# Local and global attention with a top-80 expert layer: PSUM banks by head, 32-row tiles for the global keys, longer q/k rows, and other places for the gate stage, the zeros and the late weights

## The chip, the core and the metric

The kernel runs on one core of a Trainium2 chip. The metric is the time in microseconds that one launch takes on the device; lower is better. The page called the profile is one execution of the program recorded by the hardware. In it PE is TensorE (the matrix engine), PEld its weight loads, DVE is VectorE, ACT is ScalarE, POOL is GpSimd and SP is SyncE, which here only issues transfers. L346 means line 346 of the kernel.

## What is computed

Attention comes first. In each of 8 batches, 8 heads have 32 global and 512 local tokens of width 64. A global query sees all 544 keys. A local query sees the 32 global keys and the local keys at most 32 positions away. The 4352 output rows of 512 values go through a layer of 8 experts: each token picks the expert with the largest gate logit, each expert keeps the 80 tokens with the highest gate weights, and all other rows of the output are zero.

```python
s_g = scale * q_g @ k_all.T ;  out_g = softmax(s_g) @ v_all          # k_all: global, then local keys
s_ll = where(|i - j| <= 32, scale * q_l @ k_l.T, -1e9)
s_l = concat([scale * q_l @ k_g.T, s_ll]) ;  out_l = softmax(s_l) @ concat([v_g, v_l])
x = concat([out_g, out_l]) as (8 * 544, 512)
logits = x @ w_gate ;  e = argmax(logits) ;  g = softmax(logits)[e]
for each expert e:                       # keeps its 80 largest g
    out[tok] = g[tok] * (relu(x[tok] @ w1[e]) @ w2[e])     # w1: 512 x 1024, w2: 1024 x 512
```

## The kernel before

The unit of work is a **quad**, four heads of one batch: 16 quads, two for each batch. The loop below handles quad q, while it loads, transposes and computes logits for later ones. `some(n)` runs up to n waiting steps of the top-80 search (each a VectorE maximum-of-8 and a replacement), and the functions from `La` to `Ld` form the gate stage of a finished batch. The main parts, with cuts marked by `...`:

```python
    def load_qk(q):
        b, qd = divmod(q, 2)
        qks[q] = lpool.tile([P, 2, 4, 4, D], FP32, tag="qk", name=f"qk{q}")
        for t, src in ((0, q_l), (1, k_l)):
            nc.sync.dma_start(
                out=qks[q][:, t].rearrange("p h i d -> p h (i d)"),
                in_=src[b, 4 * qd:4 * qd + 4].rearrange("h (p i) d -> p h (i d)", i=4))
    ...
    def regroup(q, t):
        if t == 0:
            qkr[q] = lpool.tile([P, 2, 4, 4, D], FP16, tag="qkr", name=f"qkr_{q}")
        nc.scalar.copy(out=qkr[q][:, t].rearrange("p i h d -> p h i d"), in_=qks[q][:, t])
    ...
    def T_chunk(q, j):
        b, qd = divmod(q, 2)
        buf = qkT[(2 * q + j) % 4]
        T_ps = psT([P, 2, 512], FP16, f"T_ps{q}_{j}")
        for t in range(2):
            for i in range(4):
                nc.tensor.transpose(out=T_ps[:, t, 128 * i:128 * i + 128],
                                    in_=qkr[q][:, t, i, 2 * j:2 * j + 2, :],
                                    identity=ident16[:, :])
        dst = buf[:, 0:1088].rearrange("x (t y) -> x t y", t=2)[:, :, 0:512]
        nc.scalar.copy(out=dst.rearrange("x t (p i) -> x t p i", i=4),
                       in_=T_ps[:].rearrange("x t (i p) -> x t p i", i=4))
        nc.scalar.copy(out=kO[(2 * q + j) % 4][:],
                       in_=buf[:, 576:1088].rearrange("x (u w y) -> x u w y", w=2, y=64)[:, :, ::-1, :])
    ...
    def L_fill(q, j):
        s = st.setdefault(q, {"eL": [], "eQ": []})
        buf = qkT[(2 * q + j) % 4]
        l_ps = [psS([P, 512], FP32, f"l_ps{q}_{j}_{hh}") for hh in range(2)]
        ko = kO[(2 * q + j) % 4]
        for t in range(8):
            for hh in range(2):
                o = 64 * hh
                if t % 2 == 0:
                    lhsT = buf[o:o + 64, 512 + 64 * t:640 + 64 * t]
                else:
                    lhsT = ko[o:o + 64, t // 2].rearrange("x w y -> x (w y)")
                nc.tensor.matmul(out=l_ps[hh][:, 64 * t:64 * t + 64], lhsT=lhsT,
                                 rhs=buf[o:o + 64, 64 * t:64 * t + 64], start=True, stop=True)
        for hh in range(2):
            eL = hpool.tile([P, 512], FP32, tag="eL", bufs=8, name=f"eL{q}_{j}_{hh}")
            nc.scalar.activation(out=eL[:], in_=l_ps[hh][:], func=AF.Exp, scale=scale)
            s["eL"].append(eL)
    ...
    def mask(q, j):
        for hh in range(2):
            eng = nc.vector if hh == 0 else nc.gpsimd
            eL = st[q]["eL"][2 * j + hh]
            eng.tensor_tensor(out=eL[:], in0=eL[:], in1=band[:].rearrange("p t i -> p (t i)"), op=ALU.mult)
    ...
    def H_chunk(q, u):
        b, qd = divmod(q, 2)
        s = st[q]
        v = vb[q % 3]
        o = psO([P, 4, 65], FP32, f"o_ps{q}_{u}")
        nc.tensor.matmul(out=o[:].rearrange("p h d -> p (h d)"), lhsT=s["eG"][:, 128 * u:128 * u + 128],
                         rhs=vbd[b % 2][:, qd].rearrange("p h d -> p (h d)"), start=True, stop=False,
                         skip_group_check=True)
        for h in range(4):
            for odd in range(2):
                t = 2 * u + odd
                nc.tensor.matmul(out=o[64 * odd:64 * odd + 64, h, :],
                                 lhsT=s["eL"][h][:, 64 * t:64 * t + 64],
                                 rhs=v[:, 5 * odd + u, h, :], start=False, stop=True,
                                 skip_group_check=True)
        rec = hpool.tile([P, 4], FP32, tag="rec", bufs=4, name="rec")
        nc.vector.reciprocal(out=rec[:], in_=o[:, :, 64])
        nc.vector.tensor_tensor(out=s["xn"][:, u].rearrange("p (h d) -> p h d", h=4), in0=o[:, :, 0:64],
                                in1=rec[:].unsqueeze(2).to_broadcast([P, 4, 64]), op=ALU.mult)
    ...
    def best(g):
        if g < 2:
            lst = spool.tile([NB * E, cap], FP32, tag="lst", bufs=1, name=f"lst{g}")
            yield from rounds(scT[g][:], lst[:])
            cand = spool.tile([E, NB, cap], FP32, tag="cand", bufs=1, name=f"cand{g}")
            def move():
                for s in range(NB):
                    nc.sync.dma_start(out=cand[:, s, :], in_=lst[8 * s:8 * s + 8, :])
            yield move
            R[g] = spool.tile([E, cap], FP32, tag=f"R{g}", bufs=1, name=f"R{g}")
            yield from rounds(cand[:].rearrange("e s r -> e (s r)"), R[g][:])
    ...
    for q in range(NQ):
        ...                                   # load_qk(q + 4), load_v(q + 2)
        H_chunk(q, 0)
        ...                                   # T_chunk(q+2, 0), La, L_fill(q+1, 0), mask, regroup, shift_v
        some(1)
        H_chunk(q, 1)
        ...                                   # Lb1, L_fill(q+1, 1), T_chunk(q+2, 1), Lb2, mask
        some(1)
        H_chunk(q, 2)
        ...                                   # Lb3, some(more), G_fill, Q_fill, regroup
        H_chunk(q, 3)
        ...                                   # Lc, some(1), Q_chunk, Q_fill, C_chunk, X_chunk x2, some(more), Ld
        if q < 4 * NRES:                      # NRES = 3 experts, a half-megabyte piece for each quad
            ...
            load_w(e, (k,))
        if q >= 1:
            zeros(1)                          # half a megabyte of the zero rows of the output
        ...                                   # from quad 14: expert 3 and half of 4, into the V buffers
```

`C_chunk` is the cast of a quad's output on GpSimd (line 392), `G_fill` and `Q_fill` compute logits with the global keys and the global queries, `shift_v` copies V moved by 64 rows, `X_chunk` transposes the output on TensorE and copies it to xT on VectorE. After the loop stand the gate stage of the last batch, what is left of the search, the final ten rounds, the threshold, the row numbers (`idx`), a gather of 80 rows for each expert, and the experts (the products `rv` and the counts `jt`, between threshold and row numbers, are in the diff below):

```python
    def fh(e):
        hTs[e] = rpool.tile([P, 8, cap], BF16, tag="fhT", bufs=2, name=f"fhT{e}")
        for half in range(2):
            h_ps = psO([P, 4, cap], FP32, f"h_ps{e}{half}")
            for f in range(4):
                for cc in range(4):
                    o = 512 * half + 128 * f
                    nc.tensor.matmul(out=h_ps[:, f, :], lhsT=w1sb[e][:, cc, o:o + 128], rhs=xTs[e][:, cc, :],
                                     start=(cc == 0), stop=(cc == 3))
            nc.scalar.activation(out=hTs[e][:, 4 * half:4 * half + 4, :], in_=h_ps[:], func=AF.Relu, scale=1.0)
    ...
        nc.gpsimd.indirect_dma_start(out=out,
                                     out_offset=bass.IndirectOffsetOnAxis(ap=idx[:, e:e + 1], axis=0),
                                     in_=y[:], in_offset=None, bounds_check=N - 1, oob_is_err=False)
```

## Time and profile before

| | us |
|---|---|
| measured time, median of three | 336.25 (335.89 to 336.62) |
| span of the profiled execution | 335.5 |
| TensorE matmuls busy | 218.9 (65%) |
| TensorE weight loads busy | 155.6 (46%) |
| VectorE busy | 207.6 (62%) |
| ScalarE busy | 146.4 (44%) |
| GpSimd busy | 149.3 (44%) |
| hardware queue (q1), share of 16 DMA engines | 44.7%, 41.30 MB, 72128 packets |
| software queue (q0), share of 16 DMA engines | 33.7%, 18.80 MB, 13984 packets |

The busy shares are means over the whole span. No engine is busy for two thirds of it, yet the shares change much from one stage to the next, so they have to be read by stage. Matmuls overlap in the array, so a TensorE that is busy isn't one at its peak. A packet is one contiguous row of a transfer: 1 KB for q and k, 256 bytes for V. The software queue is the one that GpSimd issues: weights (read as f32, written as bf16), the gather and the scatters.

### The profile page before, as it was taken

What the parts mean: (1) busy time and instruction counts of PE and PEld (TensorE: products, weight loads), DVE (VectorE), ACT (ScalarE), POOL (GpSimd) and SP (SyncE); (2) the same over time, 40 slices, a digit from 0 to 9 for tenths busy, and PEclk for the clock granted to TensorE, in tenths of its full rate; (3) what the DMA queues carried; (4) which work ended last, traced back from release to release, by engine and by line L of the source; (5) the groups of instructions that cost most, each with busy time, mean ns of one, the idle gap of its engine ahead of it and who ended that gap; (6) DMA issues with size and microseconds to landing.
All of it is one profiled execution on the core that took longest, in us unless ns stands there. A gap on an engine that the chain in (4) does not pass through costs nothing. (4 is left out here: it accounts for less than half of the span.)

```text
span 335.5 us, 8730 instructions
## 1 busy us (share of the span) xinstructions
PE 218.9 (65%) x3510; PEld 155.6 (46%) x3510; DVE 207.6 (62%) x597; ACT 146.4 (44%) x241; POOL 149.3 (44%) x200
## 2 busy tenths in 40 slices
PE   1206989887889889788684878769551013049960
PEld 0105766664666666465463456446330002047730
DVE  4303565857855675688839599989958878012320
ACT  4158977595687679375563455230000000013300
POOL 6014656763754681663644144453172125532231
PEclk9998699999999999989898599995855555559996
DMA  7787899699899899999879714204999999960211
GB/s 206 189 198 252 203 236 252 161 251 198 222 216 271 215 231 212 264 220 274 221 163 292 134 53 127 86 4 93 220 164 212 270 209 207 209 133 21 61 39 39
DMA packets 86151, 60.64 MB, mean 181 GB/s; under 512 B 50144, under 2 KB 79200, under 8 KB 86112
## 3 DMA queue, kind: packets, MB, share of 16 engines
q1 hardware_dynamic: 72128, 41.30, 44.7%
q0 software_dynamic: 13984, 18.80, 33.7%
q8 instruction: 27, 0.44, 0.5%
q14 instruction: 12, 0.10, 0.1%
HBM read 62.19 MB, written 14.70 MB: 229 GB/s over the span
## 5 line engine op out<-in xcount | busy, mean ns | idle before, releaser
L329 POOL TENSOR_TENSOR eL<-eL,band 128x512 f32<-128x512 f32 x32 | 40.9, 1278 | 42.5 <-ACT eL L322 41.0
L329 DVE TENSOR_TENSOR eL<-eL,band 128x512 f32<-128x512 f32 x32 | 27.4, 855 | 41.0 <-ACT eL L322 41.0
L275 ACT COPY qkT<-T_ps 128x1024 f16<-128x1024 f16 x32 | 32.6, 1018 | 42.9 <-PE T_ps L271 37.9
L352 PEld LDWEIGHTS o_ps<-vb,eL 128*64 128x64 f32 x1024 | 37.1, 143 | 26.1 <-issue 20.6
L352 PE MATMUL o_ps<-vb,eL 128*64 128x65 f32 x1024 | 46.5, 234 | 2.4 <-POOL vb L188 1.4
L346 PE MATMUL o_ps<-vbd,eG 128*128 128x260 f32 x128 | 45.6, 440 | 0.0
L322 ACT ACTIVATE eL<-l_ps 128x512 f32<-128x512 f32 x64 | 34.7, 597 | 9.6 <-PE l_ps L318 9.6
L145 ACT CAST qkr<-qk 128x1024 f16<-128x1024 f32 x32 | 33.4, 1046 | 12.2 <-DMA qk<-in_q_l_dram 10.7
L777 ACT ACTIVATE fhT<-h_ps 128x320 bf16<-128x320 f32 x16 | 6.9, 437 | 64.0 <-PE h_ps L775 63.6
L392 POOL CAST xb<-xn 128x1024 bf16<-128x1024 f32 x16 | 16.6, 1036 | 29.7 <-DVE xn L358 29.6
L271 PE MATMUL T_ps<-ident,qkr 128*128 128x128 f16 x256 | 22.8, 240 | 10.6 <-ACT qkr L145 7.5
L384 PE MATMUL x_ps<-identf,xn 128*128 128x128 f32 x128 | 22.1, 309 | 11.4 <-DVE xn L358 11.4
L358 DVE TENSOR_TENSOR xn<-o_ps,rec 128x256 f32<-128x256 f32 x64 | 27.2, 425 | 3.2
L283 POOL COPY qkT<-kgp 128x32 f16<-128x32 f16 x32 | 7.9, 249 | 41.2 <-ACT qkT L275 33.9
L318 PE MATMUL l_ps<-qkT 64*128 64x64 f16 x256 | 14.5, 200 | 16.1 <-POOL qkT L283 10.0
L271 PEld LDWEIGHTS <-qkr 128*128 128x128 f16 x256 | 16.9, 107 | 13.1 <-ACT qkr L145 8.6
L384 PEld LDWEIGHTS x_ps<-identf,xn 128*128 128x128 f32 x128 | 15.8, 156 | 13.9 <-DVE xn L358 13.5
L387 DVE COPY xT<-x_ps 128x512 f32<-128x512 f32 x32 | 20.6, 684 | 2.2 <-PE x_ps L384 1.9
L187 POOL COPY vb<-vb 64x1040 f32<-64x1040 f32 x16 | 17.0, 1062 | 10.4 <-DMA vb<-in_v_l_dram 10.4
L346 PEld LDWEIGHTS o_ps<-vbd,eG 128*128 128x128 f32 x128 | 20.6, 202 | 1.2
L303 ACT ACTIVATE eQ<-gq_ps 128x320 f32<-128x320 f32 x32 | 13.9, 435 | 16.6 <-PE gq_ps L300 16.5
L318 PEld LDWEIGHTS <-qkT 64*128 64x128 f16 x256 | 10.2, 99 | 22.9 <-issue 11.2
(138 smaller groups left out, 433.1 us busy)
## 6 DMA issues: line engine op xcount, KB each, us to landing
out_dram<-zt SPq DMA_DIRECT2D x17, 512.0 KB
qk<-in_q_l_dram SPq DMA_DIRECT2D x16, 512.0 KB
qk<-in_k_l_dram SPq DMA_DIRECT2D x16, 512.0 KB
w2sb<-in_moe_w_dram POOLq DMA_DIRECT2D x14, 512.0 KB, 20.8
vb<-in_v_l_dram SPq DMA_DIRECT2D x48, 128.0 KB
w1sb<-in_moe_w_dram POOLq DMA_DIRECT2D x12, 512.0 KB, 20.9
x_scr<-xb SPq DMA_DIRECT2D x8, 514.0 KB
vb<-in_moe_w_dram POOLq DMA_DIRECT2D x6, 512.0 KB, 7.2
```

Of the source, the lines that this page charges most:

```text
L145: nc.scalar.copy(out=qkr[q][:, t].rearrange("p i h d -> p h i d"), in_=qks[q][:, t])
L187: nc.gpsimd.tensor_copy(out=v[0:64, 5:9], in_=v[0:64, 1:5])
L271: nc.tensor.transpose(out=T_ps[:, t, 128 * i:128 * i + 128], in_=qkr[q][:, t, i, 2 * j:2 * j + 2, :], identity=ident16[:, :])
L275: nc.scalar.copy(out=dst.rearrange("x t (p i) -> x t p i", i=4), in_=T_ps[:].rearrange("x t (i p) -> x t p i", i=4))
L318: nc.tensor.matmul(out=l_ps[hh][:, 64 * t:64 * t + 64], lhsT=lhsT, rhs=buf[o:o + 64, 64 * t:64 * t + 64], start=True, stop=True)
L322: nc.scalar.activation(out=eL[:], in_=l_ps[hh][:], func=AF.Exp, scale=scale)
L329: eng.tensor_tensor(out=eL[:], in0=eL[:], in1=band[:].rearrange("p t i -> p (t i)"), op=ALU.mult)
L346: nc.tensor.matmul(out=o[:].rearrange("p h d -> p (h d)"), lhsT=s["eG"][:, 128 * u:128 * u + 128], rhs=vbd[b % 2][:, qd].rearrange("p h d ...
L352: nc.tensor.matmul(out=o[64 * odd:64 * odd + 64, h, :], lhsT=s["eL"][h][:, 64 * t:64 * t + 64], rhs=v[:, 5 * odd + u, h, :], start=False, ...
L358: nc.vector.tensor_tensor(out=s["xn"][:, u].rearrange("p (h d) -> p h d", h=4), in0=o[:, :, 0:64], in1=rec[:].unsqueeze(2).to_broadcast([P ...
L384: nc.tensor.transpose(out=x_ps[:, 128 * u:128 * u + 128], in_=s["xn"][:, u, 128 * j:128 * j + 128], identity=identf[:, :])
L387: nc.vector.tensor_copy(out=xT[:], in_=x_ps[:])
```

## The change

**Heads and banks.** A quad's accumulators are laid out by head instead of by block of 128 queries, one PSUM bank for each head. The global keys were one matmul over all four heads with a block-diagonal V of 260 columns; they become 16 matmuls on tiles of 32 rows of the array, each with its own 65 columns and bank. A head's outputs need only that head's masked logits, so heads 0 and 2 can start when the first half of the logits is there.

**Loads.** q and k come in rows of 2 KB (8 tokens) instead of 1 KB. w2 is read with four neighbouring rows on a partition, for which fh takes w1's columns with a step of four.

**Engines.** The kO copies go from ScalarE to GpSimd, half of the xT copies from VectorE to ScalarE; in the last quads GpSimd takes all masks and ScalarE part of the normalization.

**Gate stage and search.** The gate stage of a batch is spread over two quads. The lists of the first two groups of batches are merged before one second search, which had been done for each. The products `rv` are made for each batch in the loop.

**Late loads.** Zeros move to quads 10 and later. The weights of two and a half experts instead of one and a half go into buffers that the loop sets free (the q/k buffers, then the V buffers). The scatters are declared independent of one another.

The core of the diff, with cuts marked by `...`:

```diff
-        qks[q] = lpool.tile([P, 2, 4, 4, D], FP32, tag="qk", name=f"qk{q}")
         for t, src in ((0, q_l), (1, k_l)):
-            nc.sync.dma_start(
-                out=qks[q][:, t].rearrange("p h i d -> p h (i d)"),
-                in_=src[b, 4 * qd:4 * qd + 4].rearrange("h (p i) d -> p h (i d)", i=4))
+            hs = src[b, 4 * qd:4 * qd + 4].rearrange("(g a) (p i) d -> (a p) g (i d)", a=2, i=8)
+            nc.sync.dma_start(out=qkb[q % 2][:, t].rearrange("p g i d -> p g (i d)"), in_=hs)
     def regroup(q, t):
         if t == 0:
-            qkr[q] = lpool.tile([P, 2, 4, 4, D], FP16, tag="qkr", name=f"qkr_{q}")
-        nc.scalar.copy(out=qkr[q][:, t].rearrange("p i h d -> p h i d"), in_=qks[q][:, t])
+            qkr[q] = lpool.tile([P, 2, 8, 2, D], FP16, tag="qkr", name=f"qkr_{q}")
+        nc.scalar.copy(out=qkr[q][:, t].rearrange("p i g d -> p g i d"), in_=qkb[q % 2][:, t])
...
+    def T_chunk(q, t):
+        T_ps = psT([P, 8, 2, 64], FP16, f"T_ps{q}_{t}")
+        for i in range(8):
+            nc.tensor.transpose(out=T_ps[:, i].rearrange("x a p -> x (a p)"),
+                                in_=qkr[q][:, t, i].rearrange("p g d -> p (g d)"), identity=ident16[:, :])
+        dst = qkT[q % 2][:, :, 544 * t:544 * t + 512].rearrange("x a (p i) -> x a p i", i=8)
+        nc.scalar.copy(out=dst, in_=T_ps[:].rearrange("x i a p -> x a p i"))
+    def kg_copy(q):
+        b, qd = divmod(q, 2)
+        nc.gpsimd.tensor_copy(out=qkT[q % 2][:, :, 512:544], in_=kgp[:, b, 2 * qd:2 * qd + 2, :])
+    def kO_copy(q):
+        for a in range(2):
+            (nc.gpsimd.tensor_copy if q < 14 else nc.scalar.copy)(
+                out=kO[q % 2][:, a],
+                in_=qkT[q % 2][:, a, 576:1088].rearrange("x (u w y) -> x u w y", w=2, y=64)[:, :, ::-1, :])
...
-            s["eL"].append(eL)
+            s["eL"][2 * hh + j] = eL
 
     def mask(q, j):
         for hh in range(2):
-            eng = nc.vector if hh == 0 else nc.gpsimd
-            eL = st[q]["eL"][2 * j + hh]
+            eng = nc.gpsimd if q and (hh or q >= 12) else nc.vector
+            eL = st[q]["eL"][2 * hh + j]
             eng.tensor_tensor(out=eL[:], in0=eL[:], in1=band[:].rearrange("p t i -> p (t i)"), op=ALU.mult)
...
+    def G_all(q):
+        b, qd = divmod(q, 2)
+        s = st[q]
+        s["o"] = [psO([P, 4, 65], FP32, f"o_ps{q}_{h}") for h in range(4)]
+        for u in range(4):
+            for r in range(4):
+                h = 2 * (r % 2) + r // 2
+                nc.tensor.matmul(out=s["o"][h][:, u, :],
+                                 lhsT=s["eG"][32 * r:32 * r + 32, 128 * u:128 * u + 128],
+                                 rhs=vg[b % 2][32 * r:32 * r + 32, qd, :], start=(u == 0), stop=False,
+                                 skip_group_check=True)
+    def H_chunk(q, h):
         s = st[q]
         v = vb[q % 3]
-        o = psO([P, 4, 65], FP32, f"o_ps{q}_{u}")
-        nc.tensor.matmul(out=o[:].rearrange("p h d -> p (h d)"), lhsT=s["eG"][:, 128 * u:128 * u + 128],
-                         rhs=vbd[b % 2][:, qd].rearrange("p h d -> p (h d)"), start=True, stop=False,
-                         skip_group_check=True)
-        for h in range(4):
+        o = s["o"][h]
+        for u in range(4):
             for odd in range(2):
                 t = 2 * u + odd
-                nc.tensor.matmul(out=o[64 * odd:64 * odd + 64, h, :],
+                nc.tensor.matmul(out=o[64 * odd:64 * odd + 64, u, :],
                                  lhsT=s["eL"][h][:, 64 * t:64 * t + 64],
                                  rhs=v[:, 5 * odd + u, h, :], start=False, stop=True,
                                  skip_group_check=True)
         rec = hpool.tile([P, 4], FP32, tag="rec", bufs=4, name="rec")
         nc.vector.reciprocal(out=rec[:], in_=o[:, :, 64])
-        nc.vector.tensor_tensor(out=s["xn"][:, u].rearrange("p (h d) -> p h d", h=4), in0=o[:, :, 0:64],
-                                in1=rec[:].unsqueeze(2).to_broadcast([P, 4, 64]), op=ALU.mult)
+        if q >= 14 and h % 2:
+            for u in range(4):
+                nc.scalar.activation(out=s["xn"][:, u, 64 * h:64 * h + 64], in_=o[:, u, 0:64], func=AF.Copy,
+                                     scale=rec[:, u:u + 1])
+        else:
+            nc.vector.tensor_tensor(out=s["xn"][:, :, 64 * h:64 * h + 64], in0=o[:, :, 0:64],
+                                    in1=rec[:].unsqueeze(2).to_broadcast([P, 4, 64]), op=ALU.mult)
...
-        nc.vector.tensor_copy(out=xT[:], in_=x_ps[:])
+        if j or q >= 12:
+            nc.scalar.copy(out=xT[:], in_=x_ps[:])
+        else:
+            nc.vector.tensor_copy(out=xT[:], in_=x_ps[:])
...
+        nc.gpsimd.tensor_tensor(out=rv[:, NB * b:NB * b + NB, :, 0], in0=bs["oh"][:],
+                                in1=aw[:, NB * b:NB * b + NB].unsqueeze(2).to_broadcast([P, NB, E]), op=ALU.mult)
+        nc.gpsimd.tensor_tensor(out=rv[:, NB * b:NB * b + NB, :, 1], in0=bs["oh"][:],
+                                in1=prow[:].unsqueeze(2).to_broadcast([P, NB, E]), op=ALU.mult)
...
-            lst = spool.tile([NB * E, cap], FP32, tag="lst", bufs=1, name=f"lst{g}")
+            lst = lsts[g] = spool.tile([NB * E, cap], FP32, tag=f"lst{g}", bufs=1, name=f"lst{g}")
             yield from rounds(scT[g][:], lst[:])
-            cand = spool.tile([E, NB, cap], FP32, tag="cand", bufs=1, name=f"cand{g}")
+            if g == 0:
+                return
+            cand = spool.tile([E, NB, cap], FP32, tag="cand", bufs=1, name="cand")
             def move():
+                nc.vector.tensor_tensor(out=lst[:], in0=lst[:], in1=lsts[0][:, ::-1], op=ALU.max)
                 for s in range(NB):
                     nc.sync.dma_start(out=cand[:, s, :], in_=lst[8 * s:8 * s + 8, :])
             yield move
-            R[g] = spool.tile([E, cap], FP32, tag=f"R{g}", bufs=1, name=f"R{g}")
-            yield from rounds(cand[:].rearrange("e s r -> e (s r)"), R[g][:])
+            yield from rounds(cand[:].rearrange("e s r -> e (s r)"), fin[0:E, 0:cap])
...
-                                    in_=moe_w2[e, 512 * k:512 * k + 512].rearrange("(c p) f -> p c f", p=P))
+                                    in_=moe_w2[e, 512 * k:512 * k + 512].rearrange("(p c) f -> p c f", c=4))
...
+    NS = [[1, 1, 1, 1, 1]] * 13 + [[2, 2, 2, 2, 2]] * 3
+    NZ = [0] * 10 + [1, 1, 3, 3, 3, 3]
...
         G_chunk(q)
...
+        G_all(q)
         H_chunk(q, 0)
...
+        H_chunk(q, 2)
...
         H_chunk(q, 1)
...
         H_chunk(q, 3)
...
-        if q == NQ - 2:
-            flat = [vb[i][:].rearrange("p s h d -> p (s h d)")[:, 0:2048].bitcast(BF16) for i in (1, 2, 0)]
-            w1sb[NRES] = flat[0].rearrange("p (c f) -> p c f", c=4)
-            w2sb[NRES] = flat[1].rearrange("p (c f) -> p c f", c=8)
-            w1sb[NRES + 1] = flat[2].rearrange("p (c f) -> p c f", c=4)
+        if q == 12:
+            flat = [qkb[i][:].rearrange("p t g i d -> p (t g i d)").bitcast(BF16) for i in range(2)]
+            flat += [vb[i][:].rearrange("p s h d -> p (s h d)")[:, 0:2048].bitcast(BF16) for i in (1, 2, 0)]
+            for i, f in enumerate(flat):
+                if i % 2 == 0:
+                    w1sb[NRES + i // 2] = f.rearrange("p (c f) -> p c f", c=4)
+                else:
+                    w2sb[NRES + i // 2] = f.rearrange("p (c f) -> p c f", c=8)
             load_w(NRES, (0, 1))
+        if q == 13:
+            load_w(NRES, (2, 3))
+        if q == 14:
+            load_w(NRES + 1, (0, 1))
         if q == NQ - 1:
-            load_w(NRES, (2, 3))
-            load_w(NRES + 1, (0, 1))
+            load_w(NRES + 1, (2, 3))
+            load_w(NRES + 2, (0, 1))
+        zeros(NZ[q])
...
-    rv = rpool.tile([P, NT, E, 2], BF16, name="rv")
-    kt = keep[:].rearrange("p e t -> p t e")
-    nc.gpsimd.tensor_tensor(out=rv[:, :, :, 0], in0=kt, in1=aw[:].unsqueeze(2).to_broadcast([P, NT, E]),
-                            op=ALU.mult)
-    nc.gpsimd.tensor_tensor(out=rv[:, :, :, 1], in0=kt,
-                            in1=prow[:].unsqueeze(2).to_broadcast([P, NT, E]), op=ALU.mult)
     js = rpool.tile([P, E, NT], FP32, name="js")
     nc.vector.tensor_tensor(out=js[:], in0=keep[:], in1=pos_ps[:], op=ALU.mult)
     jt = rpool.tile([P, NT], BF16, name="jt")
-    jf = rpool.tile([P, NT], FP32, name="jf")
-    nc.vector.tensor_reduce(out=jf[:], in_=js[:].rearrange("p e t -> p t e"), axis=AX.X, op=ALU.add)
-    nc.vector.tensor_scalar(out=jt[:], in0=jf[:], scalar1=255.0, scalar2=None, op0=ALU.min)
+    with nc.allow_low_precision("small whole numbers"):
+        nc.vector.tensor_reduce(out=jt[:], in_=js[:].rearrange("p e t -> p t e"), axis=AX.X, op=ALU.add)
...
-                    o = 512 * half + 128 * f
-                    nc.tensor.matmul(out=h_ps[:, f, :], lhsT=w1sb[e][:, cc, o:o + 128], rhs=xTs[e][:, cc, :],
+                    nc.tensor.matmul(out=h_ps[:, f, :], lhsT=w1sb[e][:, cc, 512 * half + f:512 * half + 512:4], rhs=xTs[e][:, cc, :],
...
+        sc = nc.gpsimd.indirect_dma_start(out=out,
                                      out_offset=bass.IndirectOffsetOnAxis(ap=idx[:, e:e + 1], axis=0),
                                      in_=y[:], in_offset=None, bounds_check=N - 1, oob_is_err=False)
+        tc.declare_no_dep(sc.ins, group="scatters", reason="disjoint rows")
+        tc.add_to_no_dep_group("scatters", sc.ins)
```

## The prediction

> **What bounds the kernel now.** I read the span slice by slice first, then one quad (half a batch: four heads) on TensorE, then the waits, then the last 90 us. The slice view of the page:
>
> ```profile
> PE   1206989887889889788684878769551013049960
> DVE  4303565857855675688839599989958878012320
> DMA  7787899699899899999879714204999999960211
> ```
>
> Each digit is a slice of 8.4 us. There are four stages: about 30 us in which transfers arrive and TensorE has little to do; a loop to 183 us with TensorE and the DMA engines both near full; 190 to 242 us (the last four quads) with VectorE at 9 and the DMA engines at 0 to 5; then a tail to 298 us with the DMA engines full, and the experts. The cast of a finished quad on GpSimd (line 392) marks the quads: it starts at 41.9, 52.7, 64.4, 75.6, 89.8, 101.0, 113.3, 123.9, 140.0, 150.6, 166.5, 182.9, 201.4, 213.7, 229.8 and 241.7 us. Busy time between some of these marks (columns: PE, PEld, DVE, ACT, POOL, clock, DMA share, GB/s):
>
> ```profile
> 90.90:102.00 11.10, 10.09 (x199) 7.56 (x197) 7.25 (x16) 8.18 (x14) 7.20 (x10) 1.00 0.94 227
> 124.90:141.00 16.10, 12.88 (x228) 9.16 (x226) 10.86 (x37) 8.96 (x15) 6.67 (x9) 1.00 1.07 254
> 214.70:230.90 16.20, 12.39 (x190) 8.19 (x190) 14.77 (x44) 4.15 (x9) 5.70 (x7) 0.86 0.11 36
> ```
>
> The odd quads of the first half take 11 us and TensorE leads. The second row is a quad that waits for V tiles (GpSimd stood 6.07 us for a V transfer at 136 us). The third is limited by VectorE. In the TensorE timeline of the first one, matmuls follow each other but for one hole:
>
> ```profile
> 91.20 0.60 PE L346 MATMUL o_ps<-vbd,eG 128*128 128x260 f32 x2
> 91.73 0.69 PE L352 MATMUL o_ps<-vb,eL 128*64 128x65 f32 x16
> ...
> 95.27 0.19 PE L318 MATMUL l_ps<-qkT 64*128 64x64 f16 x1 [0.71 <-ACT eL L322]
> ```
>
> The four global-key matmul pairs of a quad stand 0.53 to 0.64 us apart from what follows, 2.37 us together; 16 local instructions take 0.62, or 39 ns each. The hole, some 1.3 us in all, is the second logits chunk waiting until ScalarE has emptied a bank, behind a transposed copy (1.01) and the kO copy (0.62).
>
> The tail:
>
> ```profile
> 250.00:260.00 10.00, 1.16 (x5) 0.30 (x5) 8.06 (x31) 0.24 (x1) 2.16 (x3) 0.50 1.11 210
> 260.00:270.00 10.00, 0.44 (x2) 0.12 (x2) 8.91 (x25) 0.00 (x0) 2.19 (x3) 0.50 1.18 261
> 280.00:290.00 10.00, 3.34 (x40) 2.97 (x40) 5.19 (x7) 0.00 (x0) 3.44 (x5) 0.50 1.19 209
> ...
> PE xT_ps L763 <- DMA xg<-x_scr,idx: 12.0, 1, 12.0
> ```
>
> VectorE runs top-80 rounds, but the gather, issued at 287.07, lets the experts start only at 297.84: it came through after the last weights. From 275 to 285 us weights alone move 209 GB/s as written (bf16, read as f32), and the fine slices read the same for rows of 2 KB and of 1 KB. So two chains, routing and late weights, race in the tail, and weights end last.
>
> **What the Trainium skill says.** (1) "TensorEngine Tiling (Array Packing)", Restrictions and Gotchas: row tiles may not use one PSUM bank at the same time. That is why the accumulators now go by head, one bank for each 32-row tile. No 32-row tile runs in the kernel before. (2) "TensorE: Matmul & The Clock Gate", Part 3: matmuls in different row groups run at once, and four 32-row tiles gained 3.07 times at 512 columns. Here the 64-row logits (line 318) show such overlap: 16 of them, 190 to 200 ns each, start within 0.4 us. (3) "SBUF — State Buffer", Who interferes with whom: a VectorE instruction with two SBUF inputs and a GpSimd instruction that reads SBUF shut each other out. The trace agrees: the mask on VectorE takes 680 ns at best and 1447 at worst. (4) "DMA: Bandwidth & Descriptors", Queues, rings and completion order: a ring is consumed in order. The gather shares the software queue with the weights, and the 12.0 us wait agrees.
>
> **The change, part by part.**
>
> *Global keys.* Removed: 8 instructions of 260 columns a quad, 2.37 us of TensorE. Added: 16 matmuls of 65 columns, two passes each as line 352 has them, 32 instructions; at its 39 ns that is 1.25 us. Saved 1.1 us a quad. The four banks must all be empty first, so the last head's normalization of the quad before stands ahead of it; the Q and X work between should cover that.
>
> *Moves between engines.* ScalarE loses two kO copies (1.24 us a quad) and gains one xT copy (about 0.58, from the lt copy of that shape): 8.15 to 7.5 us, and the 1.3 us hole shrinks by 0.6. GpSimd gains about 1.2 us of kO copies and small rv products: 7.2 to some 8.4. VectorE loses one xT copy, 0.68. TensorE in an odd quad: 9.9 - 1.1 - 0.6 = 8.2 us; in an even one, with the gate matmuls, 12.3 - 1.7 = 10.6. Mean 9.4, which in-order waits make about 9.8.
>
> *DMA.* A quad now moves about 1.05 MB of q/k, 0.6 V, 0.52 weights, 0.52 zeros and 0.28 x: 2.97 MB. At the 245 GB/s measured from 100 to 140 us that is 12.1 us; three quads there took 39. Without the zeros, put off to quad 10 and later, 2.45 MB or 10.0 us; half the packets for q/k should bring it to some 9.3. It falls just behind the compute, so 9.8 a quad stands for quads 1 to 9 (before: 12.1 mean to mark 9).
>
> *Start.* Mark 0 needs q/k of quads 0 to 2, two V loads, the globals and constants, about 6.15 MB; at the mean of 204 GB/s over the first 30 us that is 30 us, plus 3 of work: 33 instead of 41.9.
>
> *VectorE, late quads.* A merge of the first two groups' lists by one max removes 10 of the 60 rounds. A round on 40x512 takes 1.39 us (143.92 to 145.31), on 8x400 1.14, on 16x288 1.01. Fixed work is 4.9 us a quad: masks 1.4, reciprocals 0.7, normalization 1.7, xT 0.65, global output 0.45. Quad 10: 5 rounds, 6.9 + 4.9 + 2 for the gate = 13.5 us. Quad 11: 3 rounds, 11. From quad 12 GpSimd takes all masks and ScalarE both xT: quad 12 10.5 (GpSimd about 10); quad 13, 9 short rounds, 11.5; quad 14, 10 rounds, 11.4 + 2 + the gate's 3.5 = 17; quad 15, 10.1 + 2 = 12.5.
>
> *Marks.* 33 + 9 x 9.8 = 121 at mark 9; + 24.5 = 146 at mark 11; + 51.5 = 197 at mark 15, instead of 241.7.
>
> *Tail.* Routing, mark 15 to gather: now 45.4. Gone are the leftover rounds between 252.7 and 259.3 (6.6), the 2.6 us scalar step after the reduction (line 736) and about 0.5 of joins: 35.7, so 233. Weights: 18 half-megabyte pieces now remain after mark 15 and take until 297.8, 56 us, zeros and x among it; with four pieces loaded earlier, 14 remain: 56 x 14/18 = 43.5, so 240.5. Weights still end last.
>
> *Experts.* 297.8 to 335.5 is 37.7 us. Scatters now stand 3.4 us apart, each waiting 2.5 for the one before; once independent the last follows its y at once: - 4. Strided weight columns in w1: I allow + 1. So 240.5 + 34.7 = 275.2 of span; the measured time is 0.75 above the span: 276.
>
> **Rivals.** *GpSimd becomes the bound.* It gains work everywhere, and shares its reads with VectorE's masks. For it: 8.4 us a quad beside TensorE's 9.4, and 10 with all masks. Against it: today it idles 3 to 4 us in a clean quad. If a chain V shift, mask, kO binds, quads take 11.5: + 26 us, 302. *The transfers are hidden better than I think.* If the hole closes and 2 KB rows run as fast as the 370 to 390 GB/s seen in some slices of the first 9 us, quads take 9: - 7, and with late weights trickling into the idle DMA time the routing chain ends last, - 7 more: 262. *32-row tiles do not overlap in f32.* A 128-column f32 weight load shows 190 ns; 32 in series would be some 3 to 6 us a quad instead of 1.25, up to + 4 x 16 = 64 and no gain at all. Against it is the overlap of the 64-row tiles. *Strided w1 weight loads* lose speed: a load now repeats every 38 ns; at 100 ns, 256 of them give + 16.
>
> **Range and chances.** Quad time is uncertain by 1 us over 15 quads (15), the start by 4, the tail by 7; as roots of squares, some 17. I predict 276 us, range 257 to 297. Only the serial-tile rival reaches 330: faster 0.96, same 0.02, slower 0.02.
>
> **What would show it.** Right: marks near 33, 121, 146 and 197 us; line-392 spacing below 10 in the odd early quads; 512 global-key matmuls starting about 40 ns apart; DMA share above 0.5 between 150 and 195; experts starting within a few us of the last weight; scatters about 3 us apart. Wrong: GpSimd above 9 in the loop with TensorE waiting on its masks; global-key weight loads end to end; expert passes of clearly more than 1.3 us. The prediction falls if quads stay at 12, or the gather still waits over 12 us for weights.

## The result, and the profile after

The changed kernel takes **324.1 us** (323.3 to 327.2). The kernel before took 336.4 in the same comparison, so the ratio is 0.9635, with a 95% interval of 0.9554 to 0.9716. The forecast was 276, and 257 to 297 as its range: the sign was right, and about four fifths of the gain were missing. The profiled spans are 335.5 before and 321.5 after.

The marks (starts of the cast `xb<-xn` on GpSimd, now line 410) stand after the change at 37.1, 48.6, 59.2, 70.7, 86.4, 98.0, 109.7, 121.3, 133.1, 144.7, 162.5, 179.8, 189.4, 203.5, 223.6 and 238.2 us. Stage by stage:

| stage | before | after | change | forecast after |
|---|---|---|---|---|
| start to mark 0 | 41.9 | 37.1 | -4.8 | 33 |
| quads 1 to 9 | 108.7 | 107.5 | -1.2 | 88 |
| quads 10 and 11 | 32.3 | 35.1 | +2.8 | 24.5 |
| quads 12 to 15 | 58.8 | 58.4 | -0.4 | 51.5 |
| mark 15 to experts | 56.1 | 48.8 | -7.3 | 43.5 |
| experts | 37.7 | 34.4 | -3.3 | 34.7 |

The whole gain lies outside the loop. The fifteen quads took 199.8 us and take 201.1. The slices of the page of the changed kernel (8.0 us each):

```profile
PE   1377989679779769768759969933835024029991
DVE  4552354584674673684969287649793976001321
PEclk9999999996999999996968985985567555557997
DMA  8988898889795897898892379980899999970221
```

The DMA engines now work in most of the late slices, where they stood at 0 to 5 before. TensorE, at 8 and 9 in much of the loop before, shows mostly 6 to 9: it has less to do in quads of the same length. Windows from mark to mark (columns as in the prediction):

```profile
98.00:109.72 11.72, 9.72 (x226) 7.64 (x225) 6.68 (x22) 8.51 (x15) 8.28 (x12) 1.00 0.83 183
109.72:121.34 11.62, 8.95 (x213) 7.44 (x213) 7.59 (x20) 7.55 (x12) 8.25 (x13) 1.00 0.96 228
...
144.66:162.47 17.81, 13.15 (x229) 9.77 (x229) 12.42 (x35) 8.50 (x15) 8.39 (x11) 0.81 0.87 218
203.47:223.58 20.11, 10.17 (x213) 7.59 (x211) 12.12 (x42) 6.19 (x19) 9.68 (x13) 0.78 0.64 169
```

In the first two no engine is busy for more than 9.7 of 11.7 us, at full clock. So a chain of waits closes the quad, not one engine's work, unless it is the transfers, whose share is 0.83 and 0.96; e11 and e12 below settle that. The TensorE timeline shows where its part of the waiting is. This is the end of quad 6:

```profile
105.98 0.69 PE L362 MATMUL o_ps<-vb,eL 128*64 128x65 f32 x16
106.60 0.77 PE L383 MATMUL og<-vb,eQ 128*32 128x65 f32 x40
107.31 0.66 PE L399 MATMUL x_ps<-identf,xn 128*128 128x128 f32 x4
107.80 0.31 PE L300 MATMUL gq_ps<-qbd,qkT 128*128 128x64 f16 x5
109.76 0.63 PE L399 MATMUL x_ps<-identf,xn 128*128 128x128 f32 x4 [1.65 <-DVE xgn L390]
```

The last row is the second transpose of the attention result (X). It waits 1.65 us for `xgn`, the step on VectorE that empties `og`, the output of the global queries. The change also moves `og` from the four-bank PSUM set O to the two-bank set T, where X and the transposed scores are too; the prediction doesn't reckon with this. In the page's groups, the X transposes and the global keys of the changed kernel (busy, mean ns of one | idle of TensorE before them):

```profile
L399 PE MATMUL x_ps<-identf,xn 128*128 128x128 f32 x128 | 23.4, 312 | 36.6 <-DVE xgn L390 12.8
...
L349 PE MATMUL o_ps<-vg,eG 32*128 32x65 f32 x512 | 22.3, 322 | 0.0
```

and the X transposes of the kernel before:

```profile
L384 PE MATMUL x_ps<-identf,xn 128*128 128x128 f32 x128 | 22.1, 309 | 11.4 <-DVE xn L358 11.4
```

The idle time ahead of X went from 11.4 to 36.6 us. That is 25 us more. In quads 1 to 9 alone, before and after:

```profile
L384 PE MATMUL x_ps<-identf,xn 128*128 128x128 f32 x76 | 10.5, 278 | 1.5 <-DVE xn L358 1.5
L399 PE MATMUL x_ps<-identf,xn 128*128 128x128 f32 x72 | 11.6, 284 | 12.8 <-DVE xgn L390 6.6 <-DVE scT L504 6.2
```

There it is 1.5 against 12.8 us, and both new waits are for a VectorE step that empties a bank of set T (`scT` empties the transposed scores). The rest of the 25 us lies in the late quads. Waits of the changed kernel in quad 14, and in the tail (total, times, longest):

```profile
PE x_ps L399 <- ACT xn L370: 7.3, 1, 7.3
DVE fin L526 <- DMA cand<-lst: 6.9, 1, 6.9
...
PE xT_ps L829 <- DMA xg<-x_scr,idx: 15.9, 1, 15.9
```

The second row is VectorE standing still in the middle of a quad for a small transfer. The third is the gather, which still comes behind the weights.

### The profile page after: what moved, and what is told of

The parts are those of the page before. It is cut to its first block, busy times and chain, and to the rows that moved or that the text cites. A ratio compares the mean times of both kernels' runs of the same rounds, so it can differ in the third digit from the quotient of the medians.

```text
span 321.5 us, 9492 instructions
## 1 busy us (share of the span) xinstructions
PE 213.3 (66%) x3894; PEld 165.6 (52%) x3894; DVE 180.7 (56%) x536; ACT 145.2 (45%) x249; POOL 167.0 (52%) x224
## 4 chain that ended last, share of the span: by engine, by line
PE 37%; DVE 34%; DMA 11%; ACT 7%; issue 6%; SPq 1%; POOL 1%; POOLq 0%; DVEq 0%; ACTq 0%
PE o_ps L362 7%; PE o_ps L349 6%; DVE xn L373 5%; DMA xg<-x_scr,idx 5%; DVE eL L329 4%; PE x_ps L399 4%; ACT eL L322 4%; PE lt_ps L421 3%; PE y_ps L847 3%; PE h_ps L840 3%; PE T_ps L270 3%; DMA vb<-in_q_g_dram 3%; DVE fin L528 3%; PE l_ps L318 2%; PE lg L431 2%
## 5 line engine op out<-in xcount | busy, mean ns | idle before, releaser
L329 POOL TENSOR_TENSOR eL<-eL,band 128x512 f32<-128x512 f32 x38 | 48.0, 1271 | 54.0 <-ACT eL L322 53.7
L362 PE MATMUL o_ps<-vb,eL 128*64 128x65 f32 x1024 | 50.4, 252 | 0.0
L399 PE MATMUL x_ps<-identf,xn 128*128 128x128 f32 x128 | 23.4, 312 | 36.6 <-DVE xgn L390 12.8
L362 PEld LDWEIGHTS o_ps<-vb,eL 128*64 128x64 f32 x1024 | 41.3, 159 | 4.8 <-issue 0.4
L329 DVE TENSOR_TENSOR eL<-eL,band 128x512 f32<-128x512 f32 x26 | 22.5, 875 | 28.1 <-ACT eL L322 28.0
L145 ACT CAST qkr<-qkb 128x1024 f16<-128x1024 f32 x32 | 33.7, 1060 | 3.4 <-DMA qkb<-in_q_l_dram 3.0
L270 PE MATMUL T_ps<-ident,qkr 128*128 128x128 f16 x256 | 24.2, 252 | 8.6 <-ACT qkr L145 8.6
L367 DVE RECIPROCAL rec<-o_ps 128x4 f32<-128x4 f32 x64 | 11.1, 174 | 33.5 <-PE o_ps L362 33.3
L410 POOL CAST xb<-xn 128x1024 bf16<-128x1024 f32 x16 | 16.5, 1033 | 17.5 <-ACT xn L370 14.9
L270 PEld LDWEIGHTS <-qkr 128*128 128x128 f16 x256 | 18.0, 113 | 11.1 <-ACT qkr L145 9.1
L349 PE MATMUL o_ps<-vg,eG 32*128 32x65 f32 x512 | 22.3, 322 | 0.0
L349 PEld LDWEIGHTS o_ps<-vg,eG 32*128 32x128 f32 x512 | 19.8, 229 | 2.6 <-issue 2.4
L282 POOL COPY kO<-qkT 128x512 f16<-128x512 f16 x28 | 16.3, 610 | 8.6 <-ACT qkT L273 8.2
L403 ACT COPY xT<-x_ps 128x512 f32<-128x512 f32 x20 | 11.8, 589 | 17.7 <-PE x_ps L399 17.4
```

Of the source, the lines that this page charges most:

```text
L145: nc.scalar.copy(out=qkr[q][:, t].rearrange("p i g d -> p g i d"), in_=qkb[q % 2][:, t])
L270: nc.tensor.transpose(out=T_ps[:, i].rearrange("x a p -> x (a p)"), in_=qkr[q][:, t, i].rearrange("p g d -> p (g d)"), identity=ident16[:, :])
L349: nc.tensor.matmul(out=s["o"][h][:, u, :], lhsT=s["eG"][32 * r:32 * r + 32, 128 * u:128 * u + 128], rhs=vg[b % 2][32 * r:32 * r + 32, qd, ...
L362: nc.tensor.matmul(out=o[64 * odd:64 * odd + 64, u, :], lhsT=s["eL"][h][:, 64 * t:64 * t + 64], rhs=v[:, 5 * odd + u, h, :], start=False, ...
L399: nc.tensor.transpose(out=x_ps[:, 128 * u:128 * u + 128], in_=s["xn"][:, u, 128 * j:128 * j + 128], identity=identf[:, :])
L410: nc.gpsimd.tensor_copy(out=bst[b]["xb"][:, :, 128 * qd:128 * qd + 128].bitcast(BF16), in_=st[q]["xn"][:])
```

## The experiments

**The theories.** *Ring*: a quad is closed by logits on TensorE, exponentials on ScalarE, the mask and then the normalizations in VectorE's order, X on TensorE. Work taken off TensorE then buys nothing. *TensorE*: its own work still closes the quad. *DMA*: the transfers do. In the listing, a ratio stands against the kernel before with its interval; "base" is the kernel that the edit was made on. Times are medians of all executions and ratios those of the fast ones alone (some executions of a kernel are slower, at a lower granted clock), so where that shifts the median by over 2 us, in e3, e5 and e9, the time is that of the fast ones. The kernel before took 336.4 us beside the changed kernel but 338.6 to 339.4 beside the runs, so differences of 2 us from 324.1 are better read from the ratios; the changed kernel's is 0.9635.

### What closes quads 1 to 9

**e4_double_q**, base: the changed kernel. The loop of the global-query products runs twice; sums and numerators double, so their quotient stays.

```diff
-        for u in range(NB):
+        for u in list(range(NB)) * 2:
```

> One edit to the changed kernel: the global-query matmuls of a quad (40 instructions, 0.77 us) are issued twice, the second pass starting afresh, so the outputs stay the same. They stand where TensorE waits for VectorE. Ring theory: the extra 0.7 us a quad fits into the wait, 0 to 4 us more than 324.1. TensorE-throughput theory: 16 x 0.7 = 11 us more. DMA theory: 0 to 2 us more.

Measured: 324.0 us, 0.957 (0.950 to 0.964). The 0.7 us more a quad cost nothing, and quads 5 to 9 stay at 11.6 to 12.2. So TensorE's sum of work does not close these quads. That says nothing of the global keys (line 349): they do not stand ahead of a wait, but between X and the next logits, and the chain of the changed kernel runs through them:

```profile
109.76 0.63 PE x_ps L399 x4
110.39 1.05 PE o_ps L349 x32
111.44 0.62 PE o_ps L362 x16
...
113.61 0.61 ACT eL L322
```

So the 1.1 us saved there was on the ring. That waits added elsewhere swallowed it is inferred; no run puts the old matmul back.

**e1_og_bank**, base: the changed kernel. `og` goes back from the two-bank PSUM set T, which it shares with X, to the four-bank set O.

```diff
-        og = psT([P, 65], FP32, f"og{q}")
+        og = psO([P, 65], FP32, f"og{q}")
```

> One edit to the changed kernel: the global-query accumulator og goes back to the four-bank set O, from the two-bank set T. Ring theory (a quad is closed by a ring: logits on TensorE, exponential on ScalarE, mask and then all normalizations in order on VectorE, transposes X on TensorE): the second X no longer waits for the read of og, which takes 0.45 us on VectorE after the last normalization, so the quads get some 0.4 us shorter: 3 to 7 us less than the changed kernel's 324.1. TensorE-throughput theory: no change, within 1 us. DMA theory (loads pace the loop): no change.

Measured: 315.7 us, 0.935 (0.928 to 0.943), 8.4 below the changed kernel and more than the 3 to 7 expected. Quads 5 to 8 take 11.1 instead of 11.6 and 11.7, quad 10 takes 12.8 instead of 17.8; the idle time ahead of X in quads 1 to 9 falls from 12.8 to 6.3 us. So one PSUM bank, taken along with the move of the accumulators to banks by head, cost 8 us in all. Only the part in quads 1 to 9, 4.9 us in the two traces, is plainly the bank's. Another 6.1 lie in quads 10 and 11, but quad 10 also runs at full clock here and with less of VectorE's work in it (10.0 us against 12.4); in e11, with the same bank, it is back at 17.5 us and a clock of 0.61. What still closes a quad is in the chain of this kernel, here the end of quad 6 (start, duration, what):

```profile
99.73 0.39 PE l_ps L318 x16
100.12 0.59 ACT eL L322
...
100.74 1.31 DVE eL L329
102.05 0.10 DVE rec L367
...
102.17 0.42 DVE xn L373
102.60 0.11 DVE lmax L444
...
103.16 0.58 DVE cs L453
...
104.37 0.44 DVE xn L373
...
104.85 0.66 PE x_ps L399 x4
105.51 1.05 PE o_ps L349 x32
```

The mask of the *next* quad (line 329) and a gate step (444 to 457) lie in VectorE's queue ahead of two normalizations of *this* quad (367, 373), and X waits for these. The mask must itself wait for the exponential. That is the ring.

**e11_mask_late**, base: e1. The next quad's mask for heads 1 and 3, needed only in the middle of that quad, is issued behind the second X.

```diff
-            if q + 1 < NQ:
-                mask(q + 1, 1)
         some(NS[q][1])
...
         X_chunk(q, 1)
+        if not first and q + 1 < NQ:
+            mask(q + 1, 1)
```

> e1_og_bank with one more move: the band mask of the next quad's second half (heads 1 and 3, first needed in the middle of the next quad) is issued behind the second X instead of ahead of the normalizations of heads 1 and 3. Nothing else changes. Ring theory (exponential on ScalarE, then that mask in VectorE's queue, then the normalizations, then X): quads 2 to 11 come down from 11.1 us to 9.8-10.3, all in all 303 to 310 us against 315.7. DMA theory (the transfer engines are 91 to 94% taken in these quads, whatever the compute does): quads stay at 11.1 us, 314 to 317 us.

Measured: 312.5 us, 0.924 (0.919 to 0.930). Quads 5 to 9 alternate between 10.0 and 10.8 us, 10.3 on average and the upper edge of what the ring theory gave, but quad 10 gives back 4.7 us (17.5 against 12.8, clock 0.61 against 1.00), so the time stays above the expected 303 to 310. No instruction was removed; only the order on two queues is another.

**e12_fewer_w**, base: e11, without the weights of experts 1 and 2 (they compute with expert 0's weights).

```diff
-            load_w(e, (k,))
+            if e == 0:
+                load_w(e, (k,))
+            elif k == 0:
+                w1sb[e], w2sb[e] = w1sb[0], w2sb[0]
```

> e11_mask_late without the loads of experts 1 and 2 (2 MB read and 1 MB written a quad less in quads 4 to 11; these experts then compute with expert 0's weights, so that work is left out). DMA theory: quads 4 to 11 fall below those of e11 by the transfers' share, 1.5 us or more each, 12 us in all. Ring theory: quads as in e11 within 0.3 us; the time within 3 us of e11.

Measured: 310.5 us, 0.916 (0.910 to 0.922). In windows of equal length, e11 first (the last two columns are DMA share and GB/s):

```profile
94.30:105.40 11.10, 9.99 (x227) 7.95 (x228) 6.42 (x22) 8.28 (x14) 8.67 (x11) 1.00 0.94 212
116.50:127.60 11.10, 10.53 (x256) 8.94 (x253) 6.50 (x20) 8.39 (x15) 8.24 (x10) 1.00 0.98 222
```

and e12:

```profile
94.30:105.40 11.10, 10.72 (x245) 8.52 (x234) 7.10 (x20) 8.75 (x15) 8.57 (x13) 1.00 0.45 142
116.50:127.60 11.10, 9.99 (x228) 7.91 (x229) 7.01 (x21) 8.36 (x15) 7.90 (x11) 1.00 0.58 169
```

The DMA share falls from 0.94-0.98 to 0.45-0.58, and quads 6 to 9 keep their 10.0 and 10.8 us. The DMA theory falls for these quads. (A quad's piece of weights is 1 MB read and 0.5 MB written, half of what the expectation says. Quads 4 and 5 were longer than in e11 in this trace; why stays open.)

**e2_gate_after_x**, base: the changed kernel. The gate steps on VectorE, and the transposes of the scores, go behind the second X; their old places are empty.

```diff
         X_chunk(q, 1)
+        if late is not None:
+            Lb3(late)
+            Lc(late)
+        if pend is not None:
+            Lm(pend)
+            Lb2(pend)
```

> One edit to the changed kernel: the gate stage's VectorE steps (maximum to one-hot; normalizer to masked score; the transposes of the scores) are issued after the second X of the quad instead of between its normalizations. Ring theory: 1.7 us of an even and 2.1 us of an odd quad leave the ring and fill VectorE's idle time at the start of the next quad: quads 1 to 9 go from 11.9 to 10.3 to 11 us, 8 to 15 us less than 324.1. TensorE-throughput theory and DMA theory: within 2 us of 324.

Measured: 326.0 us, 0.961 (0.953 to 0.970), no gain. The odd quads 5, 7 and 9 fell to 10.2, 9.6 and 10.1, as the ring theory says, but quads 6 and 8 took 15.7 and 14.5. I had put a new wait into TensorE's queue:

```profile
PE t_ps L499 <- DVE sc_all L473: 4.6, 2, 2.3
```

**e6_gate_next** mends this on base e1: the same steps behind X (pairs 0 to 4), but the transposes of the scores one quad later.

```diff
         H_chunk(q, 0)
+        if lc is not None:
+            Lc(lc)
+            lc = None
...
         X_chunk(q, 1)
+        if late is not None:
+            Lb3(late)
+            lc = late
```

> The bank of e1_og_bank (og in the four-bank set) plus the gate steps of pairs 0 to 4 (maximum and scan, weights and scores) moved behind the second X of a quad; the transposes of the scores follow only in the next quad, behind H(q,0), so that TensorE's queue never stands at a score that is not there yet, which is what spoilt e2_gate_after_x. Ring theory (the quad is closed by logits, exponentials, mask, VectorE's queue, normalizations, X): odd quads come down from 11.1 to about 9.8 us, even quads stay or gain a little, 308 to 311 us in all against 315.7 for e1. If the gate steps on VectorE do not stand in the ring, 314 to 317 us.

Measured: 314.9 us, 0.934 (0.927 to 0.941), as e1. Odd quads 9.4 to 10.6, even ones 11.8: what the odd quads gain, the next even quad gives back. The last gate steps (gv 0.95, sc_all 0.98, xb 0.19) now stand ahead of that quad's first normalization, and TensorE waits another 1.0 us for the scores. Moving work on VectorE helps only where it isn't needed soon.

**e5_split_g**, base: the changed kernel. The global keys are issued in two lots, heads 0 and 2 at the quad's start, heads 1 and 3 ahead of the third local product, so that the start need not wait for all four banks.

```diff
-        G_all(q)
+        G_all(q, (0, 1))
         H_chunk(q, 0)
...
         some(NS[q][1])
+        G_all(q, (2, 3))
         H_chunk(q, 1)
```

> One edit to the changed kernel: the 16 global-key matmuls are issued in two lots of 8, heads 0 and 2 at the start of the quad, heads 1 and 3 before head 1's local matmuls, that is after the second logits chunk. Ring theory: the ring's TensorE part before that logits chunk gets some 0.4 us shorter, though two row tiles overlap less than four: 3 to 7 us less than 324.1. TensorE-throughput theory: the poorer overlap costs 0.3 to 0.5 us a quad, 4 to 8 us more. DMA theory: no change.

Measured: 335.3 us (332.0 to 336.1), 0.988 (0.983 to 0.993), 11 us worse than the changed kernel by the times and 8 by the ratios: the ring theory's sign was wrong, and the loss is at or above the upper edge of what the TensorE theory gave. One line of its TensorE timeline explains part of it:

```profile
131.78 1.11 PE L350 MATMUL o_ps<-vg,eG 32*128 32x65 f32 x16
```

16 matmuls on two row tiles take 1.11 us, as long as all 32 on four (1.05 to 1.12). So splitting them doubled their cost, to 2.2 us a quad, and the start of the ring got no shorter, which the run was built to try. Two windows of its trace, quads 5 and 7:

```profile
90.70:105.40 14.70, 13.87 (x188) 11.51 (x192) 7.14 (x18) 7.27 (x11) 8.45 (x12) 0.54 0.60 140
119.80:131.90 12.10, 9.90 (x211) 8.27 (x213) 8.02 (x21) 8.06 (x13) 8.23 (x12) 1.00 0.92 223
```

Of the quads at full clock in both kernels, 2, 7 and 8 are 3.0, 0.5 and 1.0 us longer than in the changed kernel, so TensorE's work seems to have a price at this place, unlike in e4. About half of what quads 1 to 9 lost in this trace (7.1 of 14.7 us) lies in 3, 5 and 9, whose clock reads 0.54 to 0.61 and which run at full clock in the changed kernel; why, stays open.

**e3_ko_scalar**, base: e11. The copies of the odd key windows go to ScalarE in all quads.

```diff
-            (nc.gpsimd.tensor_copy if q < 14 else nc.scalar.copy)(
+            nc.scalar.copy(
```

> e11_mask_late with the copies of the odd key windows on ScalarE in all quads instead of GpSimd in quads 0 to 13: takes some 2 us a quad off GpSimd and puts about 1 us on ScalarE. If GpSimd sets the quads, or slows VectorE's steps beside it (a mask of 0.97 us takes 1.31 to 1.45 there): quads 0.3 to 1 us shorter, 3 to 8 us below e11's 312.5. If not, ScalarE's longer queue makes the exponentials later: same to 5 us above.

Measured: 311.6 us, 0.920 (0.913 to 0.928); e11 had 0.924 (0.919 to 0.930). No gain that can be told: odd quads take 9.2 to 9.3 and even ones 11.4, 10.3 on average from 5 to 9 as in e11, so GpSimd does not set these quads.

**e17_double_q_open**, base: e14 (below), the same edit as e4.

> e14_mask_cand with the global-query products issued twice, as in e4: 0.7 us more TensorE work a quad. In the changed kernel this cost nothing (324.0 against 324.1), as the quads were closed elsewhere. If TensorE now closes the quads (9.4 us of work in 10.4), quads 2 to 9 grow by 0.5 to 0.7 us and the time by 5 to 9 us over e14's 304.8. If another wait still closes them: 304 to 307 us, quads as in e14.

Measured: 316.7 us, 0.934 (0.931 to 0.937), 11.9 above e14 and more than the 5 to 9 expected. The same 0.7 us that was free in the changed kernel costs about its own sum (16 x 0.7 = 11) once the ring is open; quads 6 to 9 go from 10.4 to 11.8 on average, while 3 to 5 stay as they were. TensorE's time has a price again here, though why it falls so unevenly was not taken apart.

### The late quads

**e7_cand**, base: e1. The top-80 rounds of quad 14 are dealt so that none stands ahead of a normalization while the candidates' transfer is under way.

```diff
-    NS = [[1, 1, 1, 1, 1]] * 13 + [[2, 2, 2, 2, 2]] * 3
+    NS = [[1, 1, 1, 1, 1]] * 13 + [[2, 2, 2, 2, 2], [0, 0, 0, 5, 5], [2, 2, 2, 2, 2]]
```

> e1_og_bank with the maximum rounds of quad 14 dealt 0,0,0,5,5 over the five places instead of 2,2,2,2,2, so that VectorE does not stand at the transfer of the candidates before this quad's normalizations. If that stand (6.9 us in the changed kernel) closes quad 14 and the late weights are issued behind it: quad 14 from 22.3 to 15-17 us, 309 to 312 us in all. If the weights already under way end last whatever quad 14 does: 314 to 317 us.

Measured: 309.5 us, 0.916 (0.907 to 0.926). Quad 14 goes from 22.3 to 15.0 us, quad 15 from 14.7 to 18.6. The stand of 6.9 us was real and half of it comes back a quad later, since the rounds still have to be done.

**e9_heat**, base: e1. During some spells of the late quads the clock column reads 0.50, and the same 32 global-key matmuls take 1.92 us instead of 1.05, as in quad 4 of the changed kernel:

```profile
71.98 1.92 PE o_ps L349 x32
```

This run issues the global-query products four times from quad 9 on, to shorten TensorE's gaps.

```diff
-        for u in range(NB):
+        for u in list(range(NB)) * (4 if q >= 9 else 1):
```

> e1_og_bank with the global-query products of quads 9 to 15 issued four times (numerators and sums both fourfold, so the quotient is unchanged): 2.1 us more TensorE work in each of seven quads, lying just ahead of the wait for the last normalization. If long waits there throw TensorE to half clock and this costs again as much as the wait: spells of half clock after quad 9 become fewer and the time falls to 308 to 313 us. If the waits alone count and the clock does not: 315 to 318 us, as the work fills time that was idle. If TensorE's own work closes these quads: 325 to 330 us.

Measured: 318.3 us (317.0 and 319.6), no faster than e1's 315.7. The spells did not become fewer: the clock of quads 10 to 15 reads 1.00, 0.77, 1.00, 0.74, 0.81 and 0.72, in e1 1.00, 0.79, 1.00, 0.88, 0.70 and 0.62. Quad 10, at 1.00 in both, took 17.4 us against 12.8. Filling gaps with work is no gain here, and it is not shown that long waits cause the spells.

**e13_all** puts the edits of e1, e11, e6 and e7 together.

> The bank of e1, the mask of e11, the gate steps of e6 and the dealt rounds of e7 together. Ring theory: odd and even quads 9.5 to 10.3 us, quad 14 about 15 us; 296 to 304 us. DMA theory: quads at 11 us on average, 308 to 312 us as in e7.

Measured: 315.0 us, 0.932 (0.925 to 0.938), above both ranges. The gains did not add: with e6's gate steps in it, quads 6 to 8 take 12.1 to 13.4. **e14_mask_cand** leaves e6 out:

> The bank of e1, the late mask of e11 and the rounds of quad 14 dealt 0,0,0,5,5 (e7). The quads before 10 and quad 14 have different closers, so the gains should add: e11 is 3.2 us below e1, e7 some 6 to 8 below it; 302 to 308 us. If the gain of e11 is given back in quad 10 as it was in part there (17.5 against 12.8 us), 306 to 310 us.

Measured: **304.8 us**, 0.899 (0.894 to 0.904), the best version of this study, and better than both kernels. TensorE's idle time ahead of X in it:

```profile
L399 PE MATMUL x_ps<-identf,xn 128*128 128x128 f32 x128 | 21.9, 296 | 6.8 <-ACT xn L370 4.4
```

6.8 us, where the changed kernel has 36.6; in quads 1 to 9 it is 2.1 against 12.8.

### The tail and the experts

**e8_undo_late**, base: the changed kernel. Same buffers, but the late weights are issued when the kernel before did it.

```diff
-            load_w(NRES, (0, 1))
-        if q == 13:
-            load_w(NRES, (2, 3))
         if q == 14:
-            load_w(NRES + 1, (0, 1))
+            load_w(NRES, (0, 1))
         if q == NQ - 1:
-            load_w(NRES + 1, (2, 3))
-            load_w(NRES + 2, (0, 1))
+            load_w(NRES, (2, 3))
+            load_w(NRES + 1, (0, 1))
...
+    load_w(NRES + 1, (2, 3))
+    load_w(NRES + 2, (0, 1))
     for e in range(NRES + 2, E):
```

> The changed kernel with its late weights kept in the same buffers, but issued when the kernel before issued them: expert 3's first half at quad 14 and second half at quad 15, expert 4's first half at quad 15, the rest after the last quad (the change: quads 12, 13, 14 and 15). If the weights end last, three pieces more of about 1 MB after mark 15 cost some 8 to 10 us: 332 to 335 us. If instead the early pieces only take the transfer engines from the loop, the time stays at 322 to 326 us.

Measured: 328.8 us, 0.977 (0.967 to 0.986), 4.7 above the changed kernel: half of what I expected. The wait for the gather is 24.2 us instead of 15.9:

```profile
PE xT_ps L828 <- DMA xg<-x_scr,idx: 24.2, 1, 24.2
```

but the experts start only 6.4 us later (293.5 against 287.1), because marks 14 and 15 came 3 us sooner in it.

**e15_w_early**, base: e14, two weight pieces issued a quad sooner.

```diff
         if q == 14:
-            load_w(NRES + 1, (0, 1))
+            load_w(NRES + 1, (0, 1, 2, 3))
         if q == NQ - 1:
-            load_w(NRES + 1, (2, 3))
             load_w(NRES + 2, (0, 1))
```

> e14_mask_cand with the two pieces of expert 4's second weights issued at the end of quad 14 instead of quad 15 (their buffer held the V of quad 14, which is free by then). If the weights after mark 15 end last at 2.4 us a piece (34.2 us for 14 pieces in the changed kernel): 4 to 5 us below e14. If the queue is still at work on earlier pieces at mark 15: 0 to 2 us.

Measured: 306.7 us, 0.907 (0.901 to 0.913): no gain. The experts start at 269.0 us, in e14 at 269.6. From mark 15 to the experts the DMA share is 1.07 (e14: 1.04), though only 0.79 to 0.80 in the quad before. That their rate counts there, and not the time of issue, fits this but isn't shown.

**e16_zeros**, base: e15. The 17 writes of zeros, from quad 10 and later, are dealt one a quad from quad 1.

```diff
-    NZ = [0] * 10 + [1, 1, 3, 3, 3, 3]
+    NZ = [0] + [1] * 11 + [2, 2, 1, 1]
```

> e15_w_early with the 17 writes of zeros (0.5 MB each) dealt one a quad from quad 1 on and two in quads 12 and 13, so that two stand in quads 14 and 15 and one after them instead of nine. If zeros take the transfer engines from the late weights: 4 to 8 us less than e15. If, in quads that are 95% taken by transfers, they make V or q/k late instead: quads 4 to 11 grow and nothing is won or some us are lost.

Measured: 309.2 us, 0.913 (0.908 to 0.918). Both expected things happened. Mark 15 to experts fell from 45.2 (e15) to 39.5 us, but the quads became

```profile
96.12:104.79 8.67, 7.40 (x169) 5.65 (x169) 4.90 (x16) 7.63 (x13) 7.88 (x11) 1.00 1.01 185
104.79:119.20 14.41, 12.32 (x266) 10.26 (x266) 8.44 (x26) 8.41 (x14) 8.43 (x11) 1.00 1.11 310
...
POOL vb L189 <- DMA vb<-in_v_l_dram: 4.8, 1, 4.8
```

8.7 and 14.4 us in turn, with V tiles late; quads 5 to 9 average 12.1 us against 10.3, and the experts took 37.6 us instead of 34.5. At the shares of e11 the transfers cost nothing that shows (e12); with half a megabyte more a quad V comes late.

**e10_undo_scat**, base: the changed kernel, with the scatters in order.

```diff
-        tc.declare_no_dep(sc.ins, group="scatters", reason="disjoint rows")
-        tc.add_to_no_dep_group("scatters", sc.ins)
```

> The changed kernel with its eight scatters of the results left in order, as the kernel before has them (each waits for the one ahead). The prediction put their independence at 4 us in the experts' stage: 327 to 328.5 us against 324.1. If the scatters hide beside the experts' products anyway: 323 to 325 us.

Measured: 331.0 us, 0.977 (0.971 to 0.984), 6.9 above by the times, 4.5 by the ratios. The experts take 38.9 us (290.1 to 329.0) instead of 34.4, so 4.5 are the scatters'; in this trace quad 8 was 3.8 longer too. The wait that came back, ahead of the scatters of `y`:

```profile
  DMA out_dram<-y,idx: 5.1, 2
```

## Why the prediction was wrong

The span was forecast at 275.2 and came out at 321.5, 46.3 us more. By its own steps:

- **Global keys, 2.37 to 1.25 us: right.** 32 instructions take 1.05 to 1.12 us at full clock. The rival of tiles that do not overlap falls.
- **TensorE 9.4 us a quad: right by luck.** The two windows above show 9.72 (even) and 8.95 (odd), a mean of 9.3, but the parts were to be 10.6 and 8.2: two errors cancel. The 12.3 that I started from in an even quad is not TensorE's work: quad 6 was 12.3 us long before, and TensorE worked 10.8 of it. And the 0.6 us by which a hole shrinks is no work to take off. TensorE's work in quads 5 and 6 fell by 1.2 and 1.1, the global keys' part alone.
- **"Which in-order waits make about 9.8": this step failed.** The quads took mostly 11.6 to 11.7 (107.5 us for nine instead of 88): **19.5 of the 46 us**, of which 5.9 are quad 4 alone (15.7 at a clock of 0.78; it holds a set-up for batches 4 to 7 and took 14.3 before, and 9.8 has no place for it). I took the busiest engine and added 0.4 for waits, because before the change that engine was nearly full (10.1 of 11.1 us). I did name the last normalization as standing ahead of the next quad's global keys, and had the Q and X work cover it; but X itself waits for the normalizations and for `xgn`. That ring is longer than TensorE's work: `og` moved into the two-bank set (0.5 us a quad, e1), and mask and gate steps stand on VectorE ahead of the normalizations (0.7 a quad for the mask alone, e11). That it lay just under the busiest engine before the change is inferred from e1, which has `og` where it was before and takes 11.1 us; the trace before gives no chain for these quads. With both opened a quad takes 10.4, of which TensorE works 9.35; e4 and e17 show the same work free in one kernel and paid in the other.
- **DMA 9.3 us a quad: too low, without harm.** In e11 the share is 0.94 to 0.98 in the windows shown, with quads of 10.0 and 10.8, so about 10. It "falls just behind the compute" as I wrote, but only just (e12, e16).
- **Quads 10 and 11, 24.5 us: 35.1 measured, 10.6 more.** VectorE's work in these two windows, 12.4 and 12.0 us, sums to my 24.5. The mistake was to take that sum for the time: the rounds lie ahead of the normalizations, X waits, and TensorE runs at a mean clock of 0.80 there. e1 gives back 6.1 us of it, with a quad 10 at full clock and with less VectorE work; what is left was not taken apart.
- **Quads 12 to 15, 51.5 us: 58.4, 6.9 more.** VectorE does not only work in quad 14, it stands 6.9 us for the candidates, with three of the quad's four normalizations behind it. My working had no transfer in it. That the two figures agree is chance: taking the stand away (e7) brought these four quads 2.1 us (60.3 to 58.2) and the tail behind them 2.8. The rest stays open.
- **Start, 33 us: 37.1, 4.1 more.** No run of its own; the 204 GB/s I used held (206, 197, 197 and 227 in the first four slices), so the 3 us allowed for work after the data was too short: on the chain the last k transfer lands at 30.2 us, and 7 us of work follow.
- **Tail, 43.5 us: 48.8, 5.3 more.** "Weights still end last" was right. Scaling 56 us by 14/18 also scaled the zeros away, though the change puts more of them behind mark 14 (nine of 17 writes, before it four); e16 took them out again and reached 39.5.
- **Experts, 34.7 us: 34.4.** Scatters -4: 4.5 in e10. The rival of slow strided w1 loads falls: a load takes 113 ns instead of 100, a pass 1.31 us as before. *GpSimd the bound* falls with e3 for the early quads, *transfers better hidden* with the quads.
- **The range** had 1 us of doubt a quad. All 15 together missed by 37 of the 46 us, and in one direction: waits on a queue that the sums left out, which I had treated as scatter. Both signs named for the prediction's fall came: quads near 12, and 15.9 us of the gather's wait.
